# A recurrence and a mixture of experts in one kernel: rows gathered half an expert sooner, expert 0's weights split two pieces ahead, the last but one expert's results turned on TensorE

## The chip, the cores and the metric

The kernel runs on one core of a Trainium2 chip. The metric is the device time of one launch in microseconds (us); the figure of a kernel is the median of its timed runs.

## The reference, cut to what matters

A linear recurrence over 4 x 768 tokens gives `x` (3072 rows of 384). Each row goes to one of 8 experts, the one with the largest logit, and through its two matrices; the result is scaled and written to the row's place.

```python
def _moe_ref(x, w_gate, w_output_gate, w1, w2) -> np.ndarray:
    N, D = x.shape
    E = w_gate.shape[1]
    logits = x @ w_gate
    e_idx = np.argmax(logits, axis=1)
...
    gate_w = probs[np.arange(N), e_idx]
    eom = 1.0 / (1.0 + np.exp(-(x @ w_output_gate)))
...
        h = np.maximum(x[mask] @ w1[e], 0.0)
        ye = h @ w2[e]
        out[mask] = gate_w[mask, None] * eom[mask, e, None] * ye
    return out.astype(np.float32)
```

w1 is 8 x 384 x 1024, w2 is 8 x 1024 x 384.

## The kernel before

**Two phases.** The first 170 us compute the recurrence chunk by chunk and route the rows: each row gets a slot in the list of its expert (`route`, L193 and L229, then a GpSimd scatter, L247, into the table `slot_table`). Then the experts follow one another. Expert 0 is done in two halves (its first 256 slots while the recurrence ends, then 192 more); experts 1 to 7 take 448, 432, 416, 400, 384, 384 and 384 columns, in an order by size that `rank_experts` finds.

**One expert** (`expert`, L623). The hidden 1024 are cut into 8 pieces f of 128. `up(f)` is 9 matmuls (L638) into `ph` (two buffers), `down(f)` 9 matmuls (L661) into three accumulators. Products are kept exact by splitting each float32 operand into a high and a low part, so each product is three matmuls: weights `whi` (ScalarE cast, L138) and `wlo` (VectorE difference, L143), rows `xh` and `xl`, hidden `hh` (ScalarE, L643) and `hl` (VectorE, L644). TensorE's order is up(0), up(1), up(2), down(0), up(3), down(1), ... up(7), down(5), down(6), down(7). Other work is hung in at hooks: (f, 0) stands right after up(f), (f, 1) after down(f-2). All five engines run their instructions in the order in which the code issues them; an instruction that waits holds up all that stand behind it on its engine.

**The weights.** A piece is loaded by SyncE (L130, 5 buffers `raw`), then split. From the second half of expert 0 on, the split is done three pieces ahead (`ahead = 3`). In the first half `ahead` is 0: pieces 0 to 2 are split before it begins, and piece f is split at hook (f, 0), that is behind `hl`(f) on VectorE, or, where the table `O` has `'pf'` above 0, at (f - pf, 0).

**The last route.** The last two tiles of rows are routed inside expert 0's first half: `O['lr']` says how many of its steps run at hook (0, 0) and how many at (1, 0); `last_places` stands at the second of these: two scatters, then the lists of slots are read back (L1026, L1028). `late` (hook (2, 1)) gathers the rows of the second half (`fetch`, L558); their transposes (L568) are the first thing TensorE does for the second half.

**The next expert's rows**, while an expert runs: `fetching` (four GpSimd gathers, `xg`) at (0, 0); `half` (L884, the two 16-bit halves of every number copied apart, one by ScalarE, one by VectorE, `pl`) at (3, 0); `rows_turned` (SyncE's transposing DMA, L890, `tT`) at (3, 1); and `join` d = 0, 1, 2 at (5, 1), (6, 0), (6, 1): ScalarE and VectorE each copy one half of a third of the rows into `xT` (L899, L900), ScalarE makes `xh` (L902), VectorE `xl` (L903). For the last expert the copies go to another order of the columns.

**The results of the expert before** (`yT`, three copies out of the accumulators). Experts 1 to 6 go `across`: their 16-bit halves are copied to `yp` at (0, 0) (L605), turned by SyncE's DMA into `yr` at (1, 0) (L609), put together by GpSimd copies `yj` (L616) at (3, 0) to (4, 1), and `put`: scaled by VectorE (`yo`, L588) and scattered by GpSimd (L590), at (3, 1), (4, 0), (4, 1), (5, 0). Expert 0's two halves go `back`: TensorE transposes them (L707) at (1, 0) to (2, 1) and `put` takes them from PSUM. The last expert's accumulators hold rows already (L658); after `nc.gpsimd.drain()` (L1067) its three puts end the program.

`yp` is set to zero once (L927, GpSimd), ahead of expert 0.

Of the kernel before, what the change touches and what calls it, by code (L numbers as in the profile page):

```python
# [24 lines left out]
E, F = 8, 1024  # L25
# [27 lines left out]
LIMIT = 2.0 ** 20  # L53


O = {'vgm': -1.61, 'vgt': -1.07, 'vg': -1.618, 'vgo': -0.703, 'score': -1.649, 'so0': -1.336, 'so1': -1.268, 'mask0': -0.673, 'mask1': -0.914, 'key': -1.529, 'ko': -1.232, 'own': -0.619, 'state': -0.175, 'sto': -0.036, 'out': 0.238, 'sums': 0.397, 'const': 2.67, 'ra': 0.72, 'rd': 0.15, 'rb': 1.282, 'lr': [2, 20], 'lp': 2, 'pf': 0, 'rn': 5, 'rz': 2.712, 'rdz': 0.18, 'sumz': 0.323, 'sc': 2.6, 'scw': 0.9, 'open': -2.721, 'ids': 2.891, 'fetch': 3.776, 'up': 0.109, 'lo': 3.433, 'upw': 6.31, 'turn0': 6.471, 'turno0': 7.577, 'turn1': 6.632, 'turno1': 8.013, 'turn2': 5.768, 'turno2': 7.737, 'warm': 15, 'sc2': 2.517, 'sc3': 5.939, 'lw': -5.962, 'lrk': -3.802, 'lv': -6.763, 'sfx': -3.687, 'pfx': -3.529, 'sk': -2.206, 'sr': -2.924, 'ruk': -3.598, 'min': 0.313, 'ed': 1, 'eu0': -1, 'ek0': -1, 'er0': -1, 'em00': -1, 'em01': 1, 'eu1': -1, 'ek1': -1, 'er1': -1, 'em10': 1, 'em11': 1, 'eu2': -1, 'ek2': -1, 'er2': -1, 'em20': 1, 'em21': -1, 'ps0': -1, 'po0': 1, 'ps1': 1, 'po1': 1, 'ps2': 1, 'po2': 1, 'ps3': 1, 'po3': 1, 'ps4': 1, 'po4': -1, 'sa0': 1, 'sa1': -1, 'sa2': 1, 'du': -1.35, 'raws': 3.402, 'w0': 4, 'w1': 0, 'wt0': 0.945, 'wn0': 2, 'wt1': -1.141, 'wn1': 0, 'wt2': -0.602, 'wn2': 0, 'wt3': 1.387, 'wn3': 0}


@with_exitstack
def tile_rwkv_moe(ctx: ExitStack, tc, rkT, wz, v_tok, vT, r_raw, k_raw, v_raw,  # L60
# [517 lines left out]
    def new_xs(pool):  # L578
        return [pool.tile([P, 3, CAP], F32R, tag=t, name=t) for t in ("xh", "xl")]
# [43 lines left out]
    def expert(e, view, idt, n, xh, xl, hooks, rows_last):  # L623
# [74 lines left out]
            else:  # L698
                nc.scalar.copy(yT[:, d, 0:nt], acc[d][:, 0:nt])

        if view >= 4:
# [185 lines left out]
    def rows_turned(key):  # L887
        pl = planes[key]
        planes[key] = pm.tile([P, 24, TM], U16, tag="tT", name="tT", bufs=1)
        nc.sync.dma_start_transpose(planes[key], pl.rearrange("p q j d -> p (q j d)"))  # L890

    def join(key, d):

        m, nt = LANES[key], WIDTHS[key]
        xT = pm.tile([P, CAP], F32, tag="xT", name="xT", bufs=2)[:, 0:nt]
        to = xT.bitcast(U16).rearrange("p (j s q) -> p q j s" if key < E - 1 else
                                       "p (s j q) -> p q j s", j=4, q=2)
        by = planes[key].rearrange("p (q j d) s -> p q d j s", q=2, j=4)[:, :, d, :, 0:m]
# [415 lines left out]
```

## Time and profile before

| what | us |
|---|---|
| median of 3 runs (437.31 to 439.97) | 438.17 |
| the profiled execution | 443.48 |
| its span on the core | 441.8 |
| TensorE busy | 392.8 |
| VectorE busy | 295.3 |
| ScalarE busy | 252.4 |
| GpSimd busy | 194.1 |

The profile is one execution, 5.3 us above the median; 1.7 us of it lie outside the span. Each row of a timeline names what the engine waited for before it, and for how long. A matmul's length in the rows is longer than the distance to the next one, because matmuls overlap: what a run of them costs is the distance of their starts. TensorE's granted clock is given as a share of its full speed.

### The profile page before, as it was taken

To read this page: it belongs to the slowest core of one execution; us is meant where nothing else is said; L and a number is where in the kernel's file an instruction comes from. 1 tells how busy PE (TensorE), PEld (TensorE's weight loads), DVE (VectorE), ACT (ScalarE), POOL (GpSimd) and SP (SyncE) were. 2 spreads that over 40 slices of the span, in tenths; PEclk is the share of its full clock that TensorE was granted. 3 is DMA by queue.
4 is the path that set the end of the run, shared out by engine and by line. 5 is a ranking of instruction groups with operands and counts; after the bars stand their busy time and mean duration, and the time that the engine had idled before them with its cause. 6 is when DMAs were issued, how large, how long until landed. Compare 5 with 4: busy or idle time off the path is not lost. (4 is left out here: it accounts for less than half of the span.)

```text
span 441.8 us, 10645 instructions
## 1 busy us (share of the span) xinstructions
PE 392.8 (89%) x4117; PEld 344.6 (78%) x4118; DVE 295.3 (67%) x527; ACT 252.4 (57%) x648; POOL 194.1 (44%) x198
## 2 busy tenths in 40 slices
PE   7199999999999995779999999998997997996990
PEld 3177777778777674669999999898997996995990
DVE  7976799799989445753564575696565655765630
ACT  1368978878978774232444674655544635756410
POOL 2314433545645743434244028248177094270252
PEclk9779999999999998899999999999899998998996
DMA  8969877788767032253356569479496595881311
GB/s 258 352 213 323 279 252 257 229 235 225 229 205 198 21 99 67 72 173 105 107 185 159 182 148 261 137 171 291 111 251 225 110 288 164 157 247 68 74 52 50
DMA packets 63244, 79.87 MB, mean 181 GB/s; under 512 B 40337, under 2 KB 44201, under 8 KB 61778
## 3 DMA queue, kind: packets, MB, share of 16 engines
q1 hardware_dynamic: 58194, 68.72, 53.0%
q0 software_dynamic: 4736, 10.28, 7.5%
q8 instruction: 34, 0.56, 0.5%
q14 instruction: 24, 0.20, 0.1%
q10 hardware_dynamic: 256, 0.11, 0.1%
HBM read 60.76 MB, written 9.84 MB: 160 GB/s over the span
## 5 line engine op out<-in xcount | busy, mean ns | idle before, releaser
L638 PE MATMUL ph<-xh,whi 128*128 128x384 f32 (+6 forms) x216 | 74.9, 347 | 4.5 <-issue 3.8
L638 PE MATMUL ph<-xh,wlo 128*128 128x384 f32 (+6 forms) x216 | 73.7, 341 | 5.2 <-DVE wlo L143 5.2
L441 POOL TENSOR_SCALAR_AFFINE_SELECT a<-a 128x512 f32<-128x512 f32 x36 | 43.2, 1213 | 78.9 <-ACT a L435 78.8
L616 POOL COPY yj<-yr 96x384 uint16<-96x384 uint16 (+4 forms) x48 | 35.2, 791 | 90.4 <-DMA yr<-yp 69.3
L643 ACT ACTIVATE hh<-ph 128x384 fp32r<-128x384 f32 (+6 forms) x72 | 34.3, 477 | 70.5 <-PE ph L638 68.9
L661 PE MATMUL acc<-hh,whi 128*128 128x384 f32 (+6 forms) x192 | 65.6, 342 | 9.3 <-ACT hh L643 5.6
L638 PE MATMUL ph<-xl,whi 128*128 128x384 f32 (+6 forms) x216 | 73.6, 341 | 0.0
L143 DVE TENSOR_TENSOR wlo<-raw,whi 128x768 fp32r<-128x768 f32 x64 | 61.0, 954 | 17.7 <-ACT whi L138 15.1
L661 PE MATMUL acc<-hl,whi 128*128 128x384 f32 (+6 forms) x192 | 66.7, 347 | 2.7 <-DVE hl L644 2.2
L661 PE MATMUL acc<-hh,wlo 128*128 128x384 f32 (+6 forms) x192 | 65.0, 339 | 0.0
L644 DVE SCALAR_TENSOR_TENSOR hl<-ph,hh 128x384 fp32r<-128x384 f32 (+6 forms) x72 | 38.5, 534 | 26.6 <-ACT hh L643 24.5
L138 ACT CAST whi<-raw 128x768 fp32r<-128x768 f32 x64 | 53.4, 835 | 0.0
L460 ACT ACTIVATE dv<-vt,dg 128x64 f32<-128x64 f32 x192 | 48.8, 363 | 0.4
L638 PEld LDWEIGHTS ph<-xh,whi 128*128 128x128 f32 x216 | 42.9, 199 | 6.5 <-issue 4.1
L638 PEld LDWEIGHTS ph<-xh,wlo 128*128 128x128 f32 x216 | 42.6, 197 | 6.9 <-DVE wlo L143 6.3
L661 PEld LDWEIGHTS acc<-hh,whi 128*128 128x128 f32 x192 | 37.2, 194 | 11.7 <-ACT hh L643 6.6
L638 PEld LDWEIGHTS ph<-xl,whi 128*128 128x128 f32 x216 | 42.7, 198 | 0.8 <-DVE xl L575 0.2
L558 POOL DMA_INDIRECT xg<-xd,idk x28 | 31.4, 1121 | 26.3 <-PE pt L568 8.2
L661 PEld LDWEIGHTS acc<-hl,whi 128*128 128x128 f32 x192 | 37.4, 195 | 5.7 <-DVE hl L644 3.8
L417 PE MATMUL pat<-rks 64*128 64x128 f32 x384 | 29.8, 292 | 10.8 <-issue 9.7
L417 PEld LDWEIGHTS pat<-rks 64*128 64x128 f32 x384 | 24.8, 193 | 18.3 <-issue 14.4
L661 PEld LDWEIGHTS acc<-hh,wlo 128*128 128x128 f32 x192 | 37.2, 194 | 0.7
(165 smaller groups left out, 742.7 us busy)
## 6 DMA issues: line engine op xcount, KB each, us to landing
raw<-in_w_dram SPq DMA_DIRECT2D x64, 384.0 KB
rks<-in_rkT_dram SPq DMA_DIRECT2D x11, 1024.0 KB
vt<-in_v_tok_dram SPq DMA_DIRECT2D x24, 256.0 KB
wts<-in_wz_dram SPq DMA_DIRECT2D x11, 516.5 KB
vs<-in_vT_dram SPq DMA_DIRECT2D x24, 192.0 KB
xd<-xt SPq DMA_DIRECT2D x24, 192.0 KB
rks<-in_rkT_dram SPq DMA_DIRECT2D x2, 512.0 KB
wts<-in_wz_dram SPq DMA_DIRECT2D x2, 258.5 KB
```

The costliest lines, as they stand in the source:

```text
L138: nc.scalar.copy(hi, raw)
L143: nc.vector.tensor_tensor(out=lo, in0=raws[e, f], in1=hi.bitcast(F32), op=ALU.subtract)
L417: nc.tensor.matmul(pats[k][q][:, p * C:(p + 1) * C], key(k, p)[rows], receptance(k, p)[rows], start=True, stop=True)
L441: nc.gpsimd.affine_select(out=a, in_=a, pattern=[[0, NP], [1, C]], compare_op=ALU.is_gt, fill=0.0, base=0, channel_multiplier=-1)
L460: nc.scalar.activation(out=dvs[k][:, p, o], in_=vts[k][:, p, VX * o:VX * o + VX], func=AF.Copy, scale=dgs[k][:, p, o:o + 1])
L558: nc.gpsimd.indirect_dma_start(out=xg[:, j, :], out_offset=None, in_=xd[0:rows, :], in_offset=bass.IndirectOffsetOnAxis(ap=idt[:, 2 * j:2 ...
L616: nc.gpsimd.tensor_copy(to[:, q], by[:, q])
L638: nc.tensor.matmul(ph[:, 0:nt], a[:, d * P:(d + 1) * P], x[:, d, 0:nt], start=k == 0, stop=k == 8)
L643: nc.scalar.activation(out=hh[:, 0:nt], in_=ph[:, 0:nt], func=AF.Relu)
L644: nc.vector.scalar_tensor_tensor(out=hl[:, 0:nt], in0=ph[:, 0:nt], scalar=0.0, in1=hh[:, 0:nt].bitcast(F32), op0=ALU.max, op1=ALU.subtract)
L661: nc.tensor.matmul(y[:, 0:nt], w[:, DM + i * P:DM + (i + 1) * P], a[:, 0:nt], start=start, stop=stop)
```

## The change

Five edits.

In the table `O`, `'lr'` goes from [2, 20] to [20, 2] and `'pf'` from 0 to 2: all steps of the last route run at hook (0, 0) of expert 0's first half, and its pieces 3 to 7 are split at hooks (1, 0) to (5, 0).

The zeroing of `yp` is cut to the columns that no result fills and moves behind the gathers of `late`. `fetching` for an expert moves into the expert before the one in which its rows are turned, to hook (6, 0) ((7, 0) of expert 0's second half for expert 2). `half` and `rows_turned` move from (3, 0) and (3, 1) to (1, 1), `join` 0 and 1 from (5, 1) and (6, 0) to (4, 1) and (5, 1); the buffers of `xh` and `xl` are taken at the first join. Expert 6's results go `back` by TensorE and no longer `across`.

```diff
@@ -698,7 +698,7 @@
-        if view >= 4:
+        if 0 < e < E - 2:
             return across(yT, view, idt)
...
@@ -906,18 +909,18 @@
-    def hooks(key, idt, backs):
+    def hooks(key, backs):
...
             if key > 1:
-                h.setdefault((0, 0), []).append(lambda: fetching(key, idt, 4))
                 for q in range(2):
-                    h.setdefault((3, 0), []).append(lambda q=q: half(key, q))
-                h.setdefault((3, 1), []).append(lambda: rows_turned(key))
+                    h.setdefault((1, 1), []).append(lambda q=q: half(key, q))
+                h.setdefault((1, 1), []).append(lambda: rows_turned(key))
                 for d in range(3):
-                    h.setdefault((5 + (d + 1) // 2, (d + 1) % 2), []).append(
-                        lambda d=d: join(key, d))
+                    h.setdefault((4 + d, 1), []).append(lambda d=d: join(key, d))
...
+        if key + 1 < E:
+            h.setdefault((6, 0) if key > 1 else (7, 0), []).append(
+                lambda: fetching(key + 1, idk[:, key + 1], 4))
         return h
 
     halves_y = [pm.tile([P, 2, 12, P], U16, tag="yp", name="yp", bufs=1)]
-    nc.gpsimd.memset(halves_y[0], 0.0)
...
     def late():
         fetching(0, early["ids"][1], 2)
+        nc.gpsimd.memset(halves_y[0][:, :, :, TM:P], 0.0)
```

Three places show what moves.

ScalarE in expert 0's first half, from the cast of the weights' piece 3 to that of piece 7 (`whi`), among the `hh` of pieces 2 to 6. Before:

```order
L643 ACTIVATE hh_3081<-ph_3071 128x256
L138 CAST whi_3103<-raw_2775 128x768
L643 ACTIVATE hh_3117<-ph_3107 128x256
L138 CAST whi_3138<-raw_2777 128x768
L643 ACTIVATE hh_3152<-ph_3142 128x256
L138 CAST whi_3167<-raw_3165 128x768
L643 ACTIVATE hh_3181<-ph_3171 128x256
L138 CAST whi_3196<-raw_3194 128x768
L643 ACTIVATE hh_3210<-ph_3200 128x256
L138 CAST whi_3244<-raw_3242 128x768
```

After:

```order
L643 ACTIVATE hh_3058<-ph_3048 128x256
L138 CAST whi_3070<-raw_2775 128x768
L643 ACTIVATE hh_3084<-ph_3074 128x256
L138 CAST whi_3088<-raw_2777 128x768
L643 ACTIVATE hh_3119<-ph_3109 128x256
L138 CAST whi_3133<-raw_3131 128x768
L643 ACTIVATE hh_3156<-ph_3146 128x256
L138 CAST whi_3162<-raw_3160 128x768
L643 ACTIVATE hh_3185<-ph_3175 128x256
L138 CAST whi_3191<-raw_3189 128x768
L643 ACTIVATE hh_3214<-ph_3204 128x256
L643 ACTIVATE hh_3254<-ph_3244 128x256
```

In the first fence the `hh` at the top is that of piece 2, in the second that of piece 1: each cast stands one `hh` sooner, two pieces of TensorE's work ahead of the `up` that reads it, and behind the last cast two `hh` follow.

VectorE in expert 5 (its `hl` have 384 columns), from the second and third of expert 4's results (`yo`) to the join of expert 6's rows (`xT`, `xl`), up to the last `hl`. Before:

```order
L588 TENSOR_SCALAR yo_5062<-yj_5042,idk_2990 100x384
L143 TENSOR_TENSOR wlo_5068<-raw_4952,whi_5067 128x768
L644 SCALAR_TENSOR_TENSOR hl_5084<-ph_5073,hh_5083 128x384
L588 TENSOR_SCALAR yo_5087<-yj_5059,idk_2990 100x384
L900 COPY xT_5101<-tT_5020 128x384
L903 TENSOR_TENSOR xl_4925<-xT_5101,xh_4924 128x384
L143 TENSOR_TENSOR wlo_5107<-raw_4981,whi_5106 128x768
L644 SCALAR_TENSOR_TENSOR hl_5123<-ph_5112,hh_5122 128x384
L900 COPY xT_5126<-tT_5020 128x384
L903 TENSOR_TENSOR xl_4925<-xT_5126,xh_4924 128x384
L900 COPY xT_5140<-tT_5020 128x384
L903 TENSOR_TENSOR xl_4925<-xT_5140,xh_4924 128x384
```

After:

```order
L588 TENSOR_SCALAR yo_5060<-yj_5040,idk_2990 100x384
L903 COPY xT_5067<-tT_4949 128x384
L906 TENSOR_TENSOR xl_5066<-xT_5067,xh_5065 128x384
L143 TENSOR_TENSOR wlo_5073<-raw_4955,whi_5072 128x768
L644 SCALAR_TENSOR_TENSOR hl_5089<-ph_5078,hh_5088 128x384
L588 TENSOR_SCALAR yo_5092<-yj_5057,idk_2990 100x384
L903 COPY xT_5106<-tT_4949 128x384
L906 TENSOR_TENSOR xl_5066<-xT_5106,xh_5065 128x384
L143 TENSOR_TENSOR wlo_5112<-raw_4984,whi_5111 128x768
L644 SCALAR_TENSOR_TENSOR hl_5128<-ph_5117,hh_5127 128x384
L903 COPY xT_5153<-tT_4949 128x384
L906 TENSOR_TENSOR xl_5066<-xT_5153,xh_5065 128x384
```

The first join passed a pair of `wlo` and `hl` and the last result; the three joins now have a pair of `wlo` and `hl` between each two and one behind the last, as that last one had before.

GpSimd at the end, in the last expert: the scatters of expert 6's results (four with `idk`; the first row is one of them, the one before it is left out) and of the last expert's (with `idl`).

```order
 L590 DMA out_dram<-yo,idk 3072x384
 L616 COPY yj<-yr 96x384 x2
-L590 DMA out_dram<-yo,idk 3072x384 x2
-L616 COPY yj<-yr 96x384 x4
-L590 DMA out_dram<-yo,idk 3072x384
-L616 COPY yj<-yr 96x384 x2
-L590 DMA out_dram<-yo,idk 3072x384
-L616 COPY yj<-yr 96x384 x2
-L590 DMA out_dram<-yo,idk 3072x384 x2
+L590 DMA out_dram<-yo,idk 3072x384 x6
 L590 DMA out_dram<-yo,idl 3072x384 x3
```

The eight copies of expert 6's results are gone; its four scatters follow directly on the last two of expert 5's.

## Rows read from the trace of the kernel before

**Rows 1.** The page: its first line and part 1's line of TensorE (busy us, share of the span, instructions).

```profile
span 441.8 us, 10645 instructions
...
PE 392.8 (89%) x4117; PEld 344.6 (78%) x4118; DVE 295.3 (67%) x527; ACT 252.4 (57%) x648; POOL 194.1 (44%) x198
```

**Rows 2.** The windows view for TensorE alone. Columns: the stretch; its length, TensorE's busy time and matmuls; the granted clock; the DMA engines' share; GB/s. The first row is expert 0's first half from its first matmul of `down` to the transposes for the second half; the others are experts 2 to 6, each from its first matmul to that of the next.

```profile
180.62:200.98 20.36, 14.40 (x101) 1.00 0.37 116
252.35:281.75 29.40, 28.75 (x145) 1.00 0.73 197
281.75:312.86 31.11, 29.02 (x146) 0.96 0.71 200
312.86:343.35 30.49, 28.18 (x146) 0.95 0.71 195
343.35:373.03 29.68, 27.06 (x146) 0.96 0.72 195
373.03:405.41 32.38, 28.01 (x145) 0.92 0.65 165
```

**Rows 3.** The windows view, all engines, for a stretch of exactly 90 matmuls out of the undisturbed middle of experts 3, 4 and 5 (416, 400 and 384 columns); after TensorE's busy time come those of the weight loads, VectorE, ScalarE and GpSimd, then the granted clock.

```profile
286.79:303.96 17.17, 17.17 (x92) 16.79 (x92) 13.67 (x33) 7.97 (x13) 10.53 (x12) 1.00 0.82 193
318.10:334.49 16.39, 16.39 (x91) 16.39 (x91) 10.10 (x17) 7.77 (x12) 10.90 (x11) 1.00 0.97 253
348.51:364.25 15.74, 15.74 (x92) 15.74 (x91) 9.62 (x17) 7.32 (x12) 10.57 (x11) 1.00 1.01 259
```

**Rows 4.** The waits view of TensorE from 174 to 431 us. Columns: who waited for which tile, what ended the wait; us in total, times, the longest.

```profile
PE acc L661 <- ACT hh L643: 5.6, 3, 3.5
PE ph L638 <- DVE wlo L143: 5.2, 5, 1.8
...
PE acc L661 <- ACT whi L138: 3.7, 2, 2.1
```

**Rows 5.** Timeline of TensorE in expert 0's first half. Columns here and below: start, length, engine, line, operation, tiles, count, and in brackets how long the engine had stood idle and what released it.

```profile
188.12 0.39 PE L638 MATMUL ph<-xh,wlo 128*128 128x256 f32 x1 [1.78 <-DVE wlo L143]
188.35 0.28 PE L638 MATMUL ph<-xh,whi 128*128 128x256 f32 x1
188.47 0.28 PE L638 MATMUL ph<-xl,whi 128*128 128x256 f32 x1
```

**Rows 6.** Timeline of VectorE, the same stretch.

```profile
180.04 1.81 DVE L188 TENSOR_SCALAR z<-z 128x2 f32<-128x2 f32 x1
...
187.12 0.95 DVE L143 TENSOR_TENSOR wlo<-raw,whi 128x768 fp32r<-128x768 f32 x1
```

**Rows 7.** Timeline of GpSimd, the same stretch.

```profile
179.17 2.66 POOL L927 MEMSET yp<- 128x3072 uint16 x1 [5.03 <-PE ph L638]
182.53 1.75 POOL L247 DMA_INDIRECT slot_table<-pair,slots  x1 [0.70 <-DVE pair L193]
...
187.77 0.59 POOL L1026 DMA_DIRECT2D ids<-slot_table  x1 [2.22 <-issue]
...
191.28 0.99 POOL L558 DMA_INDIRECT xg<-xd,ids  x1 [0.30 <-issue]
```

**Rows 8.** Timeline of VectorE in expert 5 (343.35 to 373.03 us): the third and fourth of expert 4's results, the first join, the last `hl`.

```profile
359.50 0.42 DVE L588 TENSOR_SCALAR yo<-yj,idk 100x384 f32<-100x384 f32 x1 [2.13 <-POOL yj L616]
...
362.88 0.42 DVE L588 TENSOR_SCALAR yo<-yj,idk 100x384 f32<-100x384 f32 x1 [1.62 <-POOL yj L616]
363.21 0.38 DVE L900 COPY xT<-tT 128x384 uint16<-128x384 uint16 x1
...
370.48 0.55 DVE L644 SCALAR_TENSOR_TENSOR hl<-ph,hh 128x384 fp32r<-128x384 f32 x1
```

**Rows 9.** Timeline of ScalarE in expert 5: the first join's copy and the last `hh`.

```profile
360.71 0.64 ACT L899 COPY xT<-tT 128x384 uint16<-128x384 uint16 x1 [2.06 <-DMA tT<-pl]
...
369.48 0.48 ACT L643 ACTIVATE hh<-ph 128x384 fp32r<-128x384 f32 x1
```

**Rows 10.** Timeline of TensorE: the long gaps at the ends of expert 5 and of expert 6.

```profile
370.02 0.44 PE L661 MATMUL acc<-hh,whi 128*128 128x384 f32 x1 [2.06 <-ACT whi L138]
...
401.93 0.45 PE L661 MATMUL acc<-hh,whi 128*128 128x384 f32 x1 [3.52 <-ACT hh L643]
```

**Rows 11.** Timeline of ScalarE in expert 6: one of the joins' copies for the last expert, whose rows are taken in another order.

```profile
395.68 1.93 ACT L899 COPY xT<-tT 128x384 uint16<-128x384 uint16 x1
```

**Rows 12.** Timeline of SyncE's DMA queue in expert 5.

```profile
353.89 3.35 SPq L890 DMA_TRANSPOSE tT<-pl  x1
```

**Rows 13.** Timeline of GpSimd in expert 5 (a result's scatter; the last of the gathers of the rows for expert 7) and at the end (the last of the program's scatters).

```profile
359.64 2.05 POOL L590 DMA_INDIRECT out_dram<-yo,idk  x1 [0.17 <-issue]
...
369.96 1.46 POOL L558 DMA_INDIRECT xg<-xd,idk  x1 [0.30 <-issue]
...
437.48 0.97 POOL L590 DMA_INDIRECT out_dram<-yo,idl  x1 [0.31 <-issue]
```

**Rows 14.** The instructions of line 1067. Columns: count; duration in ns, least/median/most; first and last start.

```profile
L1067 POOLq DRAIN  x1: 9089/9089/9089, 424.9 to 424.9; - x1
```

**Rows 15.** Timeline of VectorE at the end: the scaling of the last expert's last rows.

```profile
431.00 0.62 DVE L588 TENSOR_SCALAR yo<-acc,idl 128x384 f32<-128x384 f32 x1 [0.96 <-PE acc L658]
```

**Rows 16.** Timeline of TensorE in expert 0's second half: six of the transposes of line 707, and the next matmul.

```profile
206.39 0.82 PE L707 MATMUL po<-ident,yT 128*128 128x128 f32 x6
206.97 0.33 PE L638 MATMUL ph<-xh,whi 128*128 128x192 f32 x1
```

More of the change, by code (lines that the diff above doesn't have):

```diff
@@ L53 @@
 LIMIT = 2.0 ** 20
-O = {'vgm': -1.61, 'vgt': -1.07, 'vg': -1.618, 'vgo': -0.703, 'score': -1.649, 'so0': -1.336, 'so1': -1.268, 'mask0': -0.673, 'mask1': -0.914, 'key': -1.529, 'ko': -1.232, 'own': -0.619, 'state': -0.175, 'sto': -0.036, 'out': 0.238, 'sums': 0.397, 'const': 2.67, 'ra': 0.72, 'rd': 0.15, 'rb': 1.282, 'lr': [2, 20], 'lp': 2, 'pf': 0, 'rn': 5, 'rz': 2.712, 'rdz': 0.18, 'sumz': 0.323, 'sc': 2.6, 'scw': 0.9, 'open': -2.721, 'ids': 2.891, 'fetch': 3.776, 'up': 0.109, 'lo': 3.433, 'upw': 6.31, 'turn0': 6.471, 'turno0': 7.577, 'turn1': 6.632, 'turno1': 8.013, 'turn2': 5.768, 'turno2': 7.737, 'warm': 15, 'sc2': 2.517, 'sc3': 5.939, 'lw': -5.962, 'lrk': -3.802, 'lv': -6.763, 'sfx': -3.687, 'pfx': -3.529, 'sk': -2.206, 'sr': -2.924, 'ruk': -3.598, 'min': 0.313, 'ed': 1, 'eu0': -1, 'ek0': -1, 'er0': -1, 'em00': -1, 'em01': 1, 'eu1': -1, 'ek1': -1, 'er1': -1, 'em10': 1, 'em11': 1, 'eu2': -1, 'ek2': -1, 'er2': -1, 'em20': 1, 'em21': -1, 'ps0': -1, 'po0': 1, 'ps1': 1, 'po1': 1, 'ps2': 1, 'po2': 1, 'ps3': 1, 'po3': 1, 'ps4': 1, 'po4': -1, 'sa0': 1, 'sa1': -1, 'sa2': 1, 'du': -1.35, 'raws': 3.402, 'w0': 4, 'w1': 0, 'wt0': 0.945, 'wn0': 2, 'wt1': -1.141, 'wn1': 0, 'wt2': -0.602, 'wn2': 0, 'wt3': 1.387, 'wn3': 0}
@@ new lines @@
+O = {'vgm': -1.61, 'vgt': -1.07, 'vg': -1.618, 'vgo': -0.703, 'score': -1.649, 'so0': -1.336, 'so1': -1.268, 'mask0': -0.673, 'mask1': -0.914, 'key': -1.529, 'ko': -1.232, 'own': -0.619, 'state': -0.175, 'sto': -0.036, 'out': 0.238, 'sums': 0.397, 'const': 2.67, 'ra': 0.72, 'rd': 0.15, 'rb': 1.282, 'lr': [20, 2], 'lp': 2, 'pf': 2, 'rn': 5, 'rz': 2.712, 'rdz': 0.18, 'sumz': 0.323, 'sc': 2.6, 'scw': 0.9, 'open': -2.721, 'ids': 2.891, 'fetch': 3.776, 'up': 0.109, 'lo': 3.433, 'upw': 6.31, 'turn0': 6.471, 'turno0': 7.577, 'turn1': 6.632, 'turno1': 8.013, 'turn2': 5.768, 'turno2': 7.737, 'warm': 15, 'sc2': 2.517, 'sc3': 5.939, 'lw': -5.962, 'lrk': -3.802, 'lv': -6.763, 'sfx': -3.687, 'pfx': -3.529, 'sk': -2.206, 'sr': -2.924, 'ruk': -3.598, 'min': 0.313, 'ed': 1, 'eu0': -1, 'ek0': -1, 'er0': -1, 'em00': -1, 'em01': 1, 'eu1': -1, 'ek1': -1, 'er1': -1, 'em10': 1, 'em11': 1, 'eu2': -1, 'ek2': -1, 'er2': -1, 'em20': 1, 'em21': -1, 'ps0': -1, 'po0': 1, 'ps1': 1, 'po1': 1, 'ps2': 1, 'po2': 1, 'ps3': 1, 'po3': 1, 'ps4': 1, 'po4': -1, 'sa0': 1, 'sa1': -1, 'sa2': 1, 'du': -1.35, 'raws': 3.402, 'w0': 4, 'w1': 0, 'wt0': 0.945, 'wn0': 2, 'wt1': -1.141, 'wn1': 0, 'wt2': -0.602, 'wn2': 0, 'wt3': 1.387, 'wn3': 0}
@@ L871, in fetching @@
         xgs[key] = fetch(idt, n, pm)
-        xss[key] = new_xs(pm)
     def turning(key, d):
+        if d == 0:
+            xss[key] = new_xs(pm)
         m, n = xgs[key].shape[0:2]
@@ L892, in join @@
     def join(key, d):
+        if d == 0:
+            xss[key] = new_xs(pm)
         m, nt = LANES[key], WIDTHS[key]
@@ L1055, in tile_rwkv_moe @@
     load_turns()
-    backs = expert(0, 2, early["ids"][1], 2, *xss[0], hooks(1, idk[:, 1], backs), False)
+    backs = expert(0, 2, early["ids"][1], 2, *xss[0], hooks(1, backs), False)
     for e in range(1, E):
-        h = hooks(e + 1, idk[:, e + 1] if e + 1 < E else None, backs)
+        h = hooks(e + 1, backs)
         if e == 3:
```

## The prediction

> **What bounds the kernel now.** The page first: TensorE is busy for 392.8 of 441.8 us [rows 1], so only what TensorE stands idle or runs slowly for can be won. The windows by expert say where that is. Expert 0's first half takes 20.36 us for 14.40 of busy time, and experts 3 to 6 run at a granted clock of 0.92 to 0.96 while expert 2 has 1.00 [rows 2]. Ninety matmuls out of the middle of experts 3, 4 and 5 take 17.17, 16.39 and 15.74 us [rows 3]; scaled to the 144 of an expert that is 27.5, 26.2 and 25.2 (expert 6 is as wide as expert 5). The windows of rows 2 exceed this by 3.6, 4.3, 4.5 and 7.2 us, together 19.6, all at the turn from one expert to the next. The waits view names what TensorE waits for there: `hh` 5.6 us, `whi` 3.7, and in the first half `wlo` 5.2 [rows 4]. The third place is the end, where no engine computes: the last rows are scaled by 431.62 [rows 15], the last scatter ends at 438.45 [rows 13].
>
> **A. Expert 0's first half.** The waits come from a chain: `hh` of a piece, then the next `whi` on ScalarE, then `wlo` on VectorE, which `up` stands for, up to 1.78 us at once [rows 5, 6]. With `pf` = 2 the split stands two pieces ahead, its cover being some 4 us of matmuls per two pieces. Matmuls of 256 columns start 0.12 us apart [rows 5]; the 99 of the stretch need 11.9 of its 20.36 us, so 8.5 can be won. What is late next are the rows for the second half. Their last gather is issued at 191.28 + 0.99 = 192.27 [rows 7]; I allow 3 us for landing, an estimate from the 3.5 us from 357.24, the issue's end, to 360.71 for `tT` [rows 9, 12]. They would be there at 195.3, and TensorE would want them at 200.98 - 8.5 = 192.5. So the gather must come 2.8 us sooner. VectorE's L188, on two elements, takes 1.81 us while GpSimd's 2.66 us zeroing of `yp` runs (179.17 to 181.83), and the scatter waits for the chain behind it until 182.53 [rows 6, 7]. Without the zeroing ahead of it that is about 1.6 us sooner, and with all route steps ahead of `hl`(1) rather than behind it about 1.5 more: 3.1 us, just enough. I take 8.2 and allow 0.3 for the fit; bounds 5.5 (the route's move gives nothing) and 8.5.
>
> **B. The turns between experts.** I follow expert 5. VectorE waits 2.13 us at 359.50 for the third result and 1.62 at 362.88 for the fourth, and only then starts the joins, at 363.21; the last `hl` ends at 371.03, 7.8 us later, with ScalarE and VectorE waiting on each other [rows 8]. ScalarE had waited 2.06 for `tT` at 360.71, and its last `hh` ends at 369.96 [rows 9]; TensorE waits 2.06 us for it at 370.02 [rows 10] (the view names `whi`, which had ended sooner). Afterwards the first join stands behind the third result and fills the wait before the fourth. A join takes 1.6 us and a pair of `wlo` and `hl` 1.5: 359.9 + 1.6 + 1.5 + 0.4 (fourth result) + 1.6 + 1.5 + 1.6 + 1.6 = 369.7, against 371.03: 1.3 us sooner. (1.6 and 1.5 are estimates: 7.8 us hold three joins and two pairs, less small gaps.) The gap of 2.06 falls to some 0.8. The remaining 2.4 of expert 5's excess are smaller waits and matmuls at the lower of the clock's levels (1.2 and 2.4 GHz): in expert 2, where the idle time is 0.65 in all, the clock stayed at 1.00 [rows 2], so with a gap of 0.8 I give back 1.7 of it. Against that, the first two joins now stand ahead of `hh`(5) and `hh`(6), which free the two buffers `ph`: about 0.6 us of new waits at `up`(7). Gain 1.3 + 1.7 - 0.6 = 2.4. Experts 3 and 4 have wider matmuls, so more cover for the same chain: 2.7 and 3.0. Expert 6's copies take 1.93 us [rows 11] instead of 0.64 [rows 9], ScalarE's chain stays long, and of the 3.52 us gap [rows 10] and its clock I take 2.8. Expert 2's idle time, 0.6. Sum 11.5. Bounds: 20.2 (all excess and expert 2's 0.65), and 5.2 (1.3 in each of four, no clock given back).
> `half` and `rows_turned` sooner cost nothing by themselves: the gather for the next expert ends at 371.42 [rows 13], before expert 6 starts (373.03) and 5 us before its hook (1, 1). On SyncE the two transposing DMAs now stand back to back (`tT` holds the queue 3.35 us [rows 12]) and loads of weights behind them come 3 us later; the split three pieces ahead and five buffers cover that; uncovered it would cost up to 3 us an expert.
> On the port: VectorE's L188 took 1.81 us beside GpSimd's zeroing, and a scatter at 359.64 took 2.05 us while others take about 1 [rows 6, 13]. The first join now falls on that scatter. I take nothing for it; if each of five experts lost one such stretch of 1.05 us, B would be 6.2 and the time 5.3 us longer. The Trainium skill ("SBUF — State Buffer", section "Who interferes with whom") speaks against the change here: VectorE and GpSimd share a pair of ports, "and it's an exclusive lock", so a copy of VectorE blocks a GpSimd instruction for its whole length, and the other way round. The 1.81 us agree with it.
>
> **C. Expert 6's results and the end.** Twelve more transposes: six took 206.97 - 206.39 = 0.58 us of TensorE [rows 16], so 1.1 is added. What it brings is at the end. The drain takes 9.09 us from 424.9 to 434.0 [rows 14], since it follows expert 6's last scatters, which wait for `yr`'s transposing DMA and GpSimd's copies; the last three scatters wait for it. Now these scatters are issued at hooks (1, 0) to (2, 1), within the first 9 us of the last expert; a drain of 9.1 then ends by 18 of its 25.5 us, hidden under matmuls. The last scatter would end about 431.62 + 0.1 + 0.97 = 432.7 instead of 438.45: 5.7 us. Bounds: 0 and 5.75.
> The Trainium skill ("Perfetto Trace Analysis", section "Sequencer-only Instruction (DRAIN, etc)") says that the profiler shows such an instruction only from when its semaphores are satisfied. By that, the 9.09 us are the drain's own work and would move with it, as assumed; no row of before can show it.
>
> **The sum.** 8.2 + 11.5 - 1.1 + 5.7 = 24.3 us. The profiled execution of 443.48 becomes 419.2; the median of the runs shown, 5.3 us below it, goes from 438.17 to **413.9**.
>
> **The rivals.**
> *The turns gain only the earlier `hh`* (B = 5.2): the clock falls all the same, or the port stretches the joins. For it: a gap of 1.78 us in the first half left the clock at 1.00 [rows 2, 5] and one of 2.06 did not [rows 2, 10], so I can't say where it turns. Time 438.17 - 18.0 = 420.2.
> *The drain is not hidden*: it waits for the last transfers whenever it stands, and C is 0. For it: it was seen only near the end. Against it: nothing of GpSimd's stands between. Time 419.6.
> *All boundary excess goes* (B = 20.2): 405.2. Against it: expert 6's chain of 1.93 us copies.
> *The turns gain nothing* (B = 0), new waits at `up`(7) taking what the old ones give: 425.4.
> *Not faster, or slower: `tT` is late.* ScalarE stands at the first join's copy with the `whi` and `hh`(5) of the turn queued behind it, TensorE behind these. In expert 5 `tT` landed 17.4 us after the expert's start (360.71 - 343.35), from an issue at 10.5 [rows 9, 12]; now the issue should be at about 8 (an estimate: `yr` is issued from hook (1, 0), some 4 us in, and holds the queue about as long as `tT`) and the landing at 15 to 16, where VectorE is ready at 16.5 (359.9). Each us beyond that is lost in each of five experts: from 24.3 / 5 = 4.9 us beyond, at 21.4, the change gains nothing, and at 23 it loses 8 (446). Two transposing DMAs that slow each other by 6 us would do it; none in the rows took over 3.5 us to land.
>
> **How the numbers follow.** Chances: the forecast 0.58 (409 to 418, A and B each off by 3), the turns gain only part 0.15, the drain 0.11, all excess goes 0.05, the turns gain nothing 0.05, `tT` late 0.06. About 1%, 4.4 us, is what a measurement of this kernel can tell from no change: all but the last are faster by more, 0.94; the last is split, within 1% 0.03, slower 0.03. The range must leave out 0.2: 405 to 422 leaves out the last two cases, half of the 405.2 case and the tails of the forecast.
>
> **What would show it.** In the profile after: no wait for `wlo` in expert 0's first half, and that stretch near 12.2 us; the zeroing behind the gathers and L188 at some 0.2 us; granted clocks of experts 3 to 5 near 1.00 and their windows near 28.4, 27.5 and 27.3, expert 6 near 29.6; small waits at `up`(7) for `ph`; L616 and L609 gone from the last expert; the drain ended before TensorE's last matmul and the last scatter within 2 us of it. The forecast is wrong if the second half's transposes wait for `xg`, if `xT` waits for `tT` beyond 16.5 us after an expert's start, or if the drain ends after 431.

## The result, and the profile after

| | median us | runs | lowest to highest |
|---|---|---|---|
| before | 438.76 | 4 | 437.31 to 439.97 |
| after | 419.12 | 4 | 418.79 to 420.83 |

The ratio is 0.956 (0.952 to 0.960): 19.6 us faster, where 24.3 were forecast. The page of the profile after, its first line and TensorE's, which answer to [rows 1]:

```profile
span 416.8 us, 10649 instructions
...
PE 385.1 (92%) x4129; PEld 339.0 (81%) x4130; DVE 295.2 (71%) x524; ACT 251.0 (60%) x645; POOL 182.8 (44%) x190
```

TensorE's busy time fell by 7.7 us, the span by 25.0. That the span fell by more than the medians has a plain cause, shown below by a second profile of the kernel before: the first profiled execution of before was a long one, mostly in a place that the change does not touch. So the stages are compared one by one.

The windows view for TensorE, as in [rows 2]: expert 0's first half from its first `up`, its second half from its transposes together with expert 1, then experts 2 to 6, each from its first matmul, and the last row is expert 7.

```profile
167.87:185.60 17.73, 16.73 (x129) 1.00 0.45 113
185.60:241.60 56.00, 52.80 (x336) 0.97 0.56 162
241.60:269.81 28.21, 28.21 (x146) 1.00 0.74 203
269.81:298.81 29.00, 28.05 (x147) 1.00 0.73 198
298.81:326.16 27.35, 26.75 (x145) 1.00 0.80 218
326.16:353.22 27.06, 26.04 (x145) 1.00 0.80 213
353.22:383.13 29.91, 26.96 (x146) 0.97 0.73 196
383.13:410.67 27.54, 27.54 (x157) 0.97 0.10 29
```

Experts 2 to 6 took 29.40, 31.11, 30.49, 29.68 and 32.38 us [rows 2] and take 28.21, 29.00, 27.35, 27.06 and 29.91: 11.5 us less. The granted clock of experts 3 to 5 is 1.00 where it was 0.95 and 0.96; only expert 6 stays below, at 0.97 (it was 0.92).

The first two rows hold the surprise. Before, these two stretches were 26.82 (174.16 to 200.98) and 51.37 (to 252.35, where the first row of experts in [rows 2] begins). The first has lost 9.1 us, the second has gained 4.6, and its clock is 0.97. Of the 9.1 us, 1.6 belong to the part ahead of the first `down`, which ran at a clock of 0.51 in that profile of before and at 1.00 now; the stretch that the prediction counted, from the first `down` on, went from 20.36 to 12.87 us (172.73 to 185.60), where it expected some 12.2. The waits view of TensorE from 170 to 415 us says why; it answers to [rows 4]:

```profile
PE pt L568 <- DMA xg<-xd,ids: 3.1, 2, 2.9
PE acc L661 <- ACT hh L643: 2.2, 4, 1.2
PE acc L661 <- DVE hl L644: 2.1, 5, 0.5
PE ph L638 <- DVE hl L644: 1.0, 1, 1.0
...
PE ph L638 <- DVE wlo L143: 0.2, 1, 0.2
```

The waits for `whi` are gone and those for `wlo` are down to 0.2 us. At their place stands a new one, for `xg`, the rows of the second half. In TensorE's timeline it is the second transpose of that half:

```profile
185.60 0.30 PE L568 MATMUL pt<-ident,xg 96*128 96x96 f32 x1 [0.17 <-DMA xg<-xd,ids]
188.83 0.47 PE L568 MATMUL pt<-ident,xg 96*128 96x96 f32 x3 [2.92 <-DMA xg<-xd,ids]
```

The rows of the second gather were not there for 2.92 us. Behind this gap TensorE ran for a while at the lower level of its clock (granted 0.66 from 190 to 195 us): its matmuls of 256 columns start 0.21 us apart, where ahead of the gap they started 0.12 apart.

```profile
190.62 0.41 PE L661 MATMUL acc<-hh,whi 128*128 128x256 f32 x1
190.83 0.41 PE L661 MATMUL acc<-hh,wlo 128*128 128x256 f32 x1
```

The DMA view of 180 to 190 us (columns: the transfer, its queue and kind, count, KB each where one size holds, median us from issue to landing) shows what ran beside the gathers:

```profile
raw<-in_w_dram SPq DMA_DIRECT2D x5, 384.0 KB, 6.8
...
xg<-xd,ids POOLq DMA_INDIRECT x2, 5.8
```

Five loads of 384 KB of expert 1's weights, started within the same ten microseconds. The 5.8 us are the median of the two gathers, counted from the start of the issue; the second alone took 6.7.

A turn between experts, as followed in the prediction, in expert 5 (326.16 to 353.22): VectorE's third result and first join, which answer to [rows 8]; ScalarE's copy for the first join [rows 9]; TensorE's longest gap [rows 10].

```profile
341.56 0.42 DVE L588 TENSOR_SCALAR yo<-yj,idk 100x384 f32<-100x384 f32 x1 [2.12 <-POOL yj L616]
341.90 0.38 DVE L903 COPY xT<-tT 128x384 uint16<-128x384 uint16 x1
```

```profile
338.94 0.64 ACT L902 COPY xT<-tT 128x384 uint16<-128x384 uint16 x1 [1.11 <-DMA tT<-pl]
```

```profile
350.82 0.45 PE L661 MATMUL acc<-hh,whi 128*128 128x384 f32 x1 [0.52 <-ACT hh L643]
```

`tT` landed at 338.94, 12.8 us after the expert's start (it was 17.4, and 15 to 16 were expected). ScalarE then stood ready, but VectorE was still waiting for GpSimd's copy of the third result, until 341.56; the join followed it at once, as forecast. TensorE's gap fell from 2.06 to 0.52 us.

The end: the drain, which is line 1071 now [rows 14], and GpSimd's last scatter of expert 6's results, then the first and the last of expert 7's [rows 13].

```profile
L1071 POOLq DRAIN  x1: 9952/9952/9952, 392.4 to 392.4; - x1
```

```profile
394.36 0.92 POOL L590 DMA_INDIRECT out_dram<-yo,idk  x1 [0.31 <-issue]
408.44 1.01 POOL L590 DMA_INDIRECT out_dram<-yo,idl  x1 [13.16 <-DVE yo L588]
...
411.61 0.97 POOL L590 DMA_INDIRECT out_dram<-yo,idl  x1 [0.61 <-DVE yo L588]
```

The drain ran from 392.4 to 402.4, while TensorE computed until 410.67. The last scatter now ends 1.9 us behind TensorE's last matmul, not 7.5. Six of the twelve new transposes:

```profile
387.11 0.82 PE L707 MATMUL po<-ident,yT 128*96 128x128 f32 x6
```

### The profile page after: what moved, and what is told of

It is laid out like the page before. It is cut to its first block, busy times and chain, and to the rows that moved or that the text cites. A ratio compares the mean times of both kernels' runs of the same rounds, so it can differ in the third digit from the quotient of the medians.

```text
span 416.8 us, 10649 instructions
## 1 busy us (share of the span) xinstructions
PE 385.1 (92%) x4129; PEld 339.0 (81%) x4130; DVE 295.2 (71%) x524; ACT 251.0 (60%) x645; POOL 182.8 (44%) x190
## 4 chain that ended last, share of the span: by engine, by line
PE 55%; DMA 12%; DVE 10%; issue 8%; ACT 7%; POOL 6%; POOLq 0%; SPq 0%; ACTq 0%
PE ph L638 12%; PE acc L661 11%; DMA yr<-yp 5%; PE pat L417 5%; PE py L509 5%; PE py L521 4%; DVE wlo L143 3%; PE acc L658 3%; POOL yj L616 3%; DMA rks<-in_rkT_dram 3%; PE pg L385 3%; ACT whi L138 3%; PE pkt L449 3%; PE pkv L478 2%; PE py L517 2%
## 5 line engine op out<-in xcount | busy, mean ns | idle before, releaser
L638 PE MATMUL ph<-xh,whi 128*128 128x384 f32 (+6 forms) x216 | 72.9, 338 | 2.1 <-DVE hl L644 1.0
L441 POOL TENSOR_SCALAR_AFFINE_SELECT a<-a 128x512 f32<-128x512 f32 x36 | 40.8, 1148 | 77.0 <-ACT a L435 76.9
L638 PE MATMUL ph<-xh,wlo 128*128 128x384 f32 (+6 forms) x216 | 72.1, 334 | 0.4 <-DVE wlo L143 0.2
L638 PE MATMUL ph<-xl,whi 128*128 128x384 f32 (+6 forms) x216 | 72.0, 333 | 0.3 <-DVE xl L575 0.3
L661 PE MATMUL acc<-hl,whi 128*128 128x384 f32 (+6 forms) x192 | 65.4, 340 | 2.1 <-DVE hl L644 2.1
L616 POOL COPY yj<-yr 112x384 uint16<-112x384 uint16 (+4 forms) x40 | 30.4, 813 | 64.8 <-DMA yr<-yp 64.7
L638 PEld LDWEIGHTS ph<-xh,whi 128*128 128x128 f32 x216 | 41.1, 190 | 4.0 <-DVE hl L644 2.1
L638 PEld LDWEIGHTS ph<-xh,wlo 128*128 128x128 f32 x216 | 41.0, 190 | 1.7 <-DVE wlo L143 1.0
L638 PEld LDWEIGHTS ph<-xl,whi 128*128 128x128 f32 x216 | 41.1, 190 | 1.2 <-DVE xl L575 0.5
L590 POOL DMA_INDIRECT out_dram<-yo,idk x24 | 31.8, 1324 | 20.3 <-DVE yo L588 16.7
```

The lines of the kernel that those rows point to most:

```text
L441: nc.gpsimd.affine_select(out=a, in_=a, pattern=[[0, NP], [1, C]], compare_op=ALU.is_gt, fill=0.0, base=0, channel_multiplier=-1)
L590: nc.gpsimd.indirect_dma_start(out=outs[view], out_offset=bass.IndirectOffsetOnAxis(ap=idt[:, 2 * j:2 * j + 1], axis=0), in_=yo, in_offset ...
L616: nc.gpsimd.tensor_copy(to[:, q], by[:, q])
L638: nc.tensor.matmul(ph[:, 0:nt], a[:, d * P:(d + 1) * P], x[:, d, 0:nt], start=k == 0, stop=k == 8)
L661: nc.tensor.matmul(y[:, 0:nt], w[:, DM + i * P:DM + (i + 1) * P], a[:, 0:nt], start=start, stop=stop)
```

## The experiments

Twelve runs, the fourth of them the kernel before once more; ratios and intervals are to the kernel before, run in turn with each. Diffs 1 and 3 are against the kernel before, 2 and 5 to 8 against the changed kernel, 9 to 12 against that of 5.

**1. The first half's edits alone.**

```diff
-'lr': [2, 20], 'lp': 2, 'pf': 0
+'lr': [20, 2], 'lp': 2, 'pf': 2
...
-    nc.gpsimd.memset(halves_y[0], 0.0)
...
         fetching(0, early["ids"][1], 2)
+        nc.gpsimd.memset(halves_y[0][:, :, :, TM:P], 0.0)
```

> The kernel before with the first half's edits alone (all route steps at hook (0, 0), the split two pieces ahead, the zeroing of yp cut and moved). The prediction's term A stands at 8.2 us. What the profile of the changed kernel shows is another size: the matmuls of the half gain 7.5 us, and 4.6 of these are given back where the second half's transposes wait for their rows, so 2.9 us remain, and up to 1.6 more where the clock rises sooner. Theory 'given back': 3 to 4.5 us faster (about 434.5). Theory 'the give-back is the other edits' doing' (the gathers or weights that they move): about 8 us faster (430.5).

Measured: 434.10 us against 437.82, ratio 0.992 (0.989 to 0.996), so 3.3 us (1.8 to 4.9). Windows of TensorE, first half, then second half with expert 1:

```profile
169.22:186.56 17.34, 16.56 (x130) 1.00 0.47 113
186.56:242.86 56.30, 52.81 (x338) 0.97 0.55 161
```

The half takes 17.34 us, the stretch behind it 56.30 and not 51.37. The give-back comes with these edits and needs no others.

**2. The moved hooks alone** (the change without the edits of 1 and 3).

```diff
-'lr': [20, 2], 'lp': 2, 'pf': 2
+'lr': [2, 20], 'lp': 2, 'pf': 0
...
+    nc.gpsimd.memset(halves_y[0], 0.0)
...
-        nc.gpsimd.memset(halves_y[0][:, :, :, TM:P], 0.0)
...
-        if 0 < e < E - 2:
+        if view >= 4:
```

> The kernel before with the moved hooks alone (gathers, halves, transposing DMA and joins sooner). Theory 'the turns gain as summed': 11.5 us faster (about 427). Theory 'the turns only look better because the first half ends sooner': below 6 us (432 or more).

Measured: 427.45 against 437.82, ratio 0.978 (0.973 to 0.982), 9.7 us. The first theory holds within its interval (7.7 to 11.6 us).

**3. Expert 6's results on TensorE alone.**

```diff
-        if view >= 4:
+        if 0 < e < E - 2:
```

> The kernel before with expert 6's results turned on TensorE alone. The prediction's terms: 5.7 us for the hidden drain less 1.1 for twelve transposes, 4.6 us faster (434.2). The profile of the changed kernel suggests 5.6 less 2.0, 3.6 faster (435.2). If the drain waits for whatever stands at the end: 1 to 2 us slower (440).

Measured: 434.70 against 437.82, ratio 0.994 (0.991 to 0.997), 2.6 us (1.4 to 3.9): the 3.6 us of the changed profile's stages lie within that, the 4.6 of the prediction's terms do not. GpSimd's timeline, the last scatter of expert 6's results and the last of all:

```profile
413.21 0.92 POOL L590 DMA_INDIRECT out_dram<-yo,idk  x1 [0.30 <-issue]
...
430.49 0.97 POOL L590 DMA_INDIRECT out_dram<-yo,idl  x1 [0.61 <-DVE yo L588]
```

The last scatter ends at 431.46, 1.9 us behind TensorE's last matmul (429.56); the drain is hidden here too.

**4. The kernel before once more**, unchanged.

> The kernel before once more, for a second profile. The profiled execution of before took 443.48 us, its median 438.2; in the changed kernel's profile everything ahead of expert 0's first half is over 3.4 us sooner, though no edit touches it. If that is one execution's doing, this profile has the transposes of the first half near 166.3 us and not at 169.8; if an edit reaches back there, near 169.8 again.

Measured: 434.47 us, in one execution. Windows of TensorE, the same two stretches as above:

```profile
166.61:191.75 25.14, 18.70 (x130) 1.00 0.47 126
191.75:243.11 51.36, 51.08 (x338) 1.00 0.52 151
```

The first half begins at 166.61, not at 174.16, and the clock in it is 1.00 (it was 0.88 over the first profile's half, with 0.51 in its first 6.46 us). From there to expert 2 it takes 76.50 us, where the first profile took 78.19. So of the 9.0 us between the two executions 7.6 lie ahead of the change, in the recurrence, and 1.7 in these two stretches; the lateness belongs to that execution and not to the kernel.

This profile also has what the first one does not give, the landing times of the gathers (the DMA view of 180 to 186 us):

```profile
raw<-in_w_dram SPq DMA_DIRECT2D x4, 384.0 KB, 3.9
xg<-xd,ids POOLq DMA_INDIRECT x2, 5.4
```

The second gather took 6.9 us from the start of its issue (182.29) to its landing at 189.2, and TensorE took its rows at 191.75 without a wait. So the loads ran beside the gathers, and the gathers landed late, in the kernel before too; the longer first half hid it.

VectorE's timeline of this profile also shows the zeroing's neighbours again:

```profile
171.66 2.46 DVE L229 CAST slots<-slotf 128x2 int32<-128x2 f32 x1
171.74 2.38 DVE L193 RECIPROCAL pair<-z 128x2 f32<-128x2 f32 x1
```

A cast and a reciprocal of 256 numbers in 2.46 and 2.38 us, while GpSimd zeroes `yp` (171.43 to 174.10); in the profile after, beside no zeroing, the same two take 0.17 and 0.16.

**5. Expert 1's weights held until the rows have landed.**

```diff
+    hold = nc.dram_tensor("hold", (1, 2), F32, kind="Internal").ap()
+    nc.sync.dma_start(hold, xgs[0][0:1, :, 0])
     load_turns()
```

> The changed kernel, with SyncE's loads of expert 1's weights held until the rows for expert 0's second half have landed (a DMA of eight bytes out of those rows stands ahead of them in SyncE's queue). Theory 'contention': the two gathers took 3.8 and 5.7 us to land because five loads of 384 KB, started 1.3 us after the first gather, share the DMA engines; without them they land in about 2.5 to 3 us, and TensorE's wait of 2.9 us and what follows it shrink: 3 to 4 us faster than the changed kernel (415.5). Theory 'the lists are late': the gather is issued too late anyway and its landing is its own: no change (419).

Measured: 414.90 us, ratio 0.946 (0.942 to 0.949), 4.2 us faster than the changed kernel. The same DMA view (180 to 190 us), and the windows of the first half and of what follows:

```profile
xg<-xd,ids POOLq DMA_INDIRECT x2, 3.6
```

```profile
169.04:186.52 17.48, 16.76 (x130) 0.98 0.32 77
186.52:237.89 51.37, 51.09 (x339) 1.00 0.64 189
```

The gathers land in 3.6 us from their issue (the median of the two again), not 5.8, no wait for `xg` is left, and the second stretch is back at 51.37 us, to the hundredth what it was before. The held loads are the only edit, so it was the loads that had stretched the gathers. All profiles with landing times agree: the second gather took 6.1 to 7.5 us from the start of its issue in the seven with the loads beside it (after and 1 to 4, 6, 7), and 2.8 to 3.6 us in the six with the loads held (5, 8 to 12).

**6. The first join ahead of the third result.**

```diff
-                    h.setdefault((4 + d, 1), []).append(lambda d=d: join(key, d))
+                    h.setdefault((4 + d, 1), []).insert(0, lambda d=d: join(key, d))
```

> The changed kernel with the first join ahead of the third result at hook (4, 1), and not behind it. In experts 5 and 6 the turned rows had landed at 338.94 and 367.58, and VectorE stood 2.1 us for GpSimd's copy of the third result before it took the join, at 341.90 and 369.13. Theory 'the results' chain on GpSimd sets the joins': 1.5 us in each of four turns, 5 to 6 us faster than the changed kernel (413.5). Theory 'the joins' own chain sets them': under 1.5 us (418), since the results then come later on GpSimd and the next gather with them.

Measured: 418.93 us, ratio 0.958 (0.951 to 0.966): nothing to tell from the changed kernel's 0.956. VectorE and ScalarE in expert 5:

```profile
341.22 0.38 DVE L903 COPY xT<-tT 128x384 uint16<-128x384 uint16 x1
...
343.84 0.42 DVE L588 TENSOR_SCALAR yo<-yj,idk 100x384 f32<-100x384 f32 x1 [1.04 <-POOL yj L616]
...
346.36 0.42 DVE L588 TENSOR_SCALAR yo<-yj,idk 100x384 f32<-100x384 f32 x1 [0.58 <-POOL yj L616]
```

```profile
343.49 0.84 ACT L138 CAST whi<-raw 128x768 fp32r<-128x768 f32 x1 [1.28 <-DMA raw<-in_w_dram]
```

The join starts sooner, at 341.22 in an expert that began 1.9 us later than above. But VectorE now waits 1.04 us for the third result behind it and 0.58 for the fourth, which stands ahead of the second join, and ScalarE waits 1.28 us for a weight load. The wait went over to the next instruction that depends on GpSimd. The five to six us that I expected were wrong.

**7. The rows turned at the old hooks, the joins at the new.**

```diff
-                    h.setdefault((1, 1), []).append(lambda q=q: half(key, q))
-                h.setdefault((1, 1), []).append(lambda: rows_turned(key))
+                    h.setdefault((3, 0), []).append(lambda q=q: half(key, q))
+                h.setdefault((3, 1), []).append(lambda: rows_turned(key))
```

> The changed kernel with the halves and the transposing DMA back at hooks (3, 0) and (3, 1), the joins left at their new places. The rival of the prediction that ends slower: rows turned too late for the first join. By its price the rows land 17 to 18 us after an expert's start, 1 to 1.5 us after VectorE is ready, which costs 1 to 1.5 us in each of four turns: 4 to 6 us slower than the changed kernel (424). If the move of the halves was worth nothing: 419.

Measured: 424.69 us, ratio 0.971 (0.965 to 0.978), 5.6 us slower than the changed kernel. The waits view of TensorE (190 to 400 us), and ScalarE's first join copy in expert 5, which here began at 329.77:

```profile
PE ph L638 <- DVE hl L644: 7.3, 4, 3.2
```

```profile
346.39 0.63 ACT L902 COPY xT<-tT 128x384 uint16<-128x384 uint16 x1 [4.95 <-DMA tT<-pl]
```

ScalarE stands 4.95 us for `tT`, which lands 16.6 us after the start, with `hh` behind it, and TensorE waits for buffers `ph`: 7.3 us in four waits. This is the mechanism of the prediction's rival "`tT` is late", made to happen; the kernel is still faster than the one before, but moving `half` and `rows_turned` is worth these 5.6 us. The rival's price was too low: counted from when VectorE is ready, 16.5 us after the expert's start, a landing at 16.6 would cost 0.5 us in five experts. ScalarE stood at its copy from 341.44 on, 11.7 us after the start. How much of the 5.6 us is the later `half` on ScalarE and VectorE, and not the landing, stays open.

**8. Both 5 and 6.**

> The changed kernel with both, the weights held and the first join ahead. If the two are independent: the sum of the two single gains, 8 to 10 us faster than the changed kernel (410).

Measured: 415.35 us, ratio 0.944 (0.937 to 0.951): the gain of 5 alone.

**9. The weights held, and the results one hook later.**

```diff
-            [((3 + (j + 1) // 2, (j + 1) % 2),
+            [(((4, 0), (4, 1), (5, 0), (6, 0))[j],
               lambda j=j: put(view + j, idt, j, got[1, j])) for j in range(4)]
```

> The changed kernel with the weights held (414.9 us measured) and the results of the expert before put one hook later: at (4, 0), (4, 1), (5, 0) and (6, 0), so that VectorE does not stand for GpSimd's copies of the third and fourth result ahead of the joins. With the first join alone moved ahead, that wait only went over to the results behind it (1.04 and 0.58 us in expert 5). Theory 'VectorE's waits for the results set the joins': the waits of TensorE for hh and for the buffers ph in the turns go, 2 to 3 us faster than with the weights held alone (412.5). Theory 'the joins and splits themselves fill both engines': within 1 us (414 to 416).

Measured: 413.74 us, ratio 0.940 (0.934 to 0.946). It is the fastest kernel here and beats both the one before and the changed one; against 5 (0.946, 0.942 to 0.949) it can't be told apart: its own runs go from 407.85 to 415.11. Between the two theories it decides nothing. In the turns TensorE's waits for the buffers `ph` (0.9 us in 5) are gone and those for `hh` are 1.5 us in place of 2.1.

**10. The weights held, the split not ahead.**

```diff
-'lr': [20, 2], 'lp': 2, 'pf': 2
+'lr': [20, 2], 'lp': 2, 'pf': 0
```

> The changed kernel with the weights held and the split of expert 0's pieces not ahead (pf back at 0). By the prediction's term A, the waits for wlo return, some 7 of the 8.5 us (the rest is the route's place): the first half's stretch from its first up near 24 us in place of 17.5, the time 421 to 422. If the route's place and the zeroing did it: 415.

Measured: 424.02 us, ratio 0.970 (0.964 to 0.975), 9.1 us slower than 5, more than the 421 to 422 expected. Windows and the wait that returned:

```profile
167.79:193.56 25.77, 20.28 (x130) 0.90 0.36 87
193.56:244.93 51.37, 51.09 (x339) 1.00 0.58 171
```

```profile
PE ph L638 <- DVE wlo L143: 4.7, 5, 1.8
```

The half is 8.3 us longer (25.77 against 17.48) and the rest is untouched. Of the 8.3, 0.9 lie ahead of the first `down`, where the granted clock was 0.50 to 0.65 in this execution. Behind it, the stretch that the prediction counted takes 19.85 us against 12.41: 7.4 us, of 8.2 forecast, with the rows out of the way.

**11. The weights held, `yp` zeroed whole and early.**

```diff
+    nc.gpsimd.memset(halves_y[0], 0.0)
...
-        nc.gpsimd.memset(halves_y[0][:, :, :, TM:P], 0.0)
```

> The changed kernel with the weights held and yp zeroed whole and early, as before. GpSimd's zeroing of some 2.7 us again stands ahead of the two last scatters and, by the row of before, blocks a small VectorE instruction for 1.8 us. The prediction gave the move 1.6 us of lateness: the last scatter some 1.5 to 2 us later, the rows then land after TensorE wants them, 1 to 2 us slower than with the weights held alone (416.5). If it hides behind the route: 415.

Measured: 419.63 us, ratio 0.956 (0.950 to 0.962), 4.7 us slower than 5, more than expected. The windows of the two stretches, then GpSimd, and VectorE's `pair`, for which the scatter used to wait:

```profile
170.51:189.99 19.48, 17.04 (x130) 1.00 0.27 61
189.99:244.22 54.23, 52.88 (x337) 0.97 0.61 182
```

```profile
176.28 2.66 POOL L931 MEMSET yp<- 128x3072 uint16 x1 [4.39 <-DMA xd<-xt]
179.09 1.00 POOL L247 DMA_INDIRECT slot_table<-pair,slots  x1 [0.15 <-issue]
```

```profile
175.32 0.16 DVE L193 RECIPROCAL pair<-z 128x2 f32<-128x2 f32 x1
```

`pair` was ready by 175.5, the scatter started at 179.09. The zeroing stood ahead of it on GpSimd and itself waited 4.39 us, by its row for the last write of the recurrence's rows `xt` (the pool that holds `yp` opens where the recurrence's pool closes). The other two profiles with the early zeroing name other releasers ([rows 7] and experiment 4), so why it waits is not settled; in all three it starts 4.8 to 5.8 us behind the half's first `up`. No VectorE instruction was blocked in this execution (a `wlo` and an `hl` within the zeroing took their usual 0.96 and 0.42 us): the price is the place in the queue. The issue of the second gather ends 18.92 us behind the half's first `up`, where it ends 15.32 behind it in 5, 3.6 us sooner; the two stretches are 4.9 us longer.

**12. The weights held, the route's steps at (1, 0) again.**

```diff
-'lr': [20, 2], 'lp': 2, 'pf': 2
+'lr': [2, 20], 'lp': 2, 'pf': 2
```

> The changed kernel with the weights held and most steps of the last route back at hook (1, 0), the split still two pieces ahead and the zeroing still behind. The prediction gave the route's place 1.5 us of the rows' lateness. With the weights held the rows landed 0.3 us before TensorE wanted them, so if the route's place counts, its pair and scatters come 1.5 to 2 us later and the time is 1.5 to 2 us longer than with the weights held alone (414.9): about 416.5. If the route's steps wait for TensorE or ScalarE anyway: 415.

Measured: 416.63 us, ratio 0.949 (0.942 to 0.956), which overlaps that of 5. The windows of the two stretches decide it:

```profile
172.32:189.70 17.38, 16.65 (x130) 1.00 0.34 77
189.70:241.05 51.35, 51.07 (x339) 1.00 0.65 189
```

17.38 and 51.35 us against 17.48 and 51.37, and the second gather's issue ends 15.41 us behind the half's first `up`, against 15.32: the route's place is worth nothing once the zeroing is out of the way. The difference of the medians lies elsewhere; the profile has the half begin at 172.32, where that of 5 has 169.04.

## Why the prediction was right, and where it was off

**A, 8.2 us forecast, 3.3 measured (experiment 1).** The half itself came near the sum: its counted stretch is 7.5 us shorter, and experiment 10 puts the split ahead at 7.4. The step that failed is "I allow 3 us for landing", and what the prediction named as a sign of being wrong, that the second half's transposes wait for `xg`, came true. The last gather came sooner as wanted: its issue ends 15.25 us behind the half's first `up` (183.12), where it ended 18.11 behind it in the first profile of before and 16.67 in experiment 4. But its rows landed at 188.8, 5.7 us after that, since the loads of expert 1's weights ran beside it. The prediction looked for what is late next, named the gather, and took its landing from a transfer with nothing beside it. It didn't ask what already runs beside the gather: the kernel before has these loads too, and in experiment 4 the same gather landed 5.9 us after the end of its issue. There the half ended 8.5 us after that issue (8.7 in the first profile, 200.98 against 192.27 [rows 2, 7]), which covered the slow landing. The price was 2.92 us of waiting and matmuls at the lower clock behind it, 4.6 in all; experiment 5 gives 4.2 back, and with the loads held the landing took 1.9 us from the issue's end.

**The zeroing.** Its lateness was put at 1.6 us, by the blocked L188 [rows 6]. Experiment 11 says 3.6, and 4.7 in time, by another way: the instruction holds up the scatters behind it. `pair` was ready by 175.5, the zeroing still waited until 176.28 and then took 2.66 us. The block is real (1.81 us [rows 6], 2.46 in experiment 4), as the Trainium skill ("SBUF — State Buffer", section "Who interferes with whom") says of the shared pair of ports, but it isn't what cost most. The route's place, put at 1.5 us, is worth nothing (experiment 12). That the two errors nearly cancelled, 3.1 us forecast together and 3.7 by these two experiments, was luck.

**B, 11.5 forecast, 9.7 measured alone (experiment 2), 11.5 by the windows.** Expert by expert 1.2, 2.1, 3.1, 2.6 and 2.5 us against 0.6, 2.7, 3.0, 2.4 and 2.8. The walk through expert 5 held: the first join stands behind the third result, the gap of 2.06 us became 0.52 and the clock came back. The rival "the clock falls all the same" is refuted by the windows of experts 3 to 5. The new waits for `ph`, put at 0.6 us in each turn, came in one expert alone (1.0 us, in expert 6). The port, weighed at up to 5.3 us against the change, took nothing that the windows show, though two of GpSimd's copies (L616) took 2.03 us at 343.16, beside the first join's end and a `wlo`, where the two before took 1.16. That the joins can be sooner still was tried twice (6, 9) and gave at most a little: by experiment 6's rows the waits went over to the later results and to a load.

**C, 5.7 less 1.1 forecast, 2.6 measured alone (experiment 3).** The distance from TensorE's last matmul to the last scatter's end fell by 5.6 us, as forecast, and six transposes took 0.57 us, as before. Two things were left out. Expert 7 takes 27.54 us, not 25.55: 1.1 are the transposes, and most of the rest are matmuls at the lower clock at its start, after expert 6's gaps (granted 0.68 over the first 2.87 us; before, 0.92 over the first 2.59). And the span ends 4.2 us after the last scatter, where it ended 3.3 after it. That the drain is its own work, as the Trainium skill ("Perfetto Trace Analysis", section "Sequencer-only Instruction (DRAIN, etc)") let one think, is borne out in part. Its row took 9.09 us before and 9.95 now, but it begins 2.0 and 2.8 us before the last scatter ahead of it ends, so in that much of the row a scatter still ran. The rest moved with the scatters: both times the drain ended 7.1 us after the end of that scatter (426.90 to 433.99, 395.28 to 402.35), and so it did in all fourteen profiles.

**The sum.** 3.3 + 9.7 + 2.6 = 15.6 us by single parts, 19.6 together. Each has an interval of some 1.3 to 2 us, so the difference of 4.0 us is at the edge of what they allow. Whether the parts help each other stays open; the stages of the changed kernel, 11.5 for B, 5.6 less 2.0 and 0.9 for the end, and 2.8 to 4.5 for A with either profile of before, give 17.0 to 18.7. The median alone could not have told which step failed: the rival "the drain is not hidden" had 419.6, and 419.12 came of the late rows while the drain was hidden. With the loads held (experiment 5) the time is 414.9, where 413.9 was forecast, so the landing is 4.2 of the 5.2 us by which the forecast was off.

## What to carry to other kernels

When a stage is made to end sooner, look for the small transfer that the next stage waits for and ask what runs beside it: a landing that was slow all along shows only when the slack in front of it is gone. A dependence of eight bytes can put the loads behind it. An off-path instruction at the head of an in-order queue costs its own wait besides its length. And before the spans of two profiles are subtracted, look whether the stages ahead of the change agree.

## What was not expected of the hardware

The second of two gathers of 96 rows landed 2.8 to 3.6 us after the start of its issue with the large loads held, and 6.1 to 7.5 us after it with loads of 384 KB beside it. A GpSimd drain behind indirect scatters ends 7.1 us after the last of them, in all fourteen profiles. In two executions of the kernel before, the recurrence ahead of the experts differed by 7.6 us (first half begun at 166.61 and at 174.16); what made it differ was not looked into.
